# Quarters of the array for four first-layer blocks and three token tiles of an attention and GELU kernel

## The chip, the cores and the metric

The kernel runs on one core of one Trainium2 chip. The metric is the device time of one launch in microseconds; lower is better. A core has several engines, each with a queue of its own that runs in order and waits on semaphores: TensorE (PE; its weight loads are listed apart as PEld) multiplies matrices into the accumulation memory PSUM, ScalarE (ACT) applies functions such as exponential and gelu, VectorE (DVE) does sums, products and copies, GpSimd (POOL) does slower elementwise work and issues some DMAs, and SyncE (SP) issues most DMAs. PSUM has eight banks, and one bank holds 512 float32 columns on 128 partitions.

## The reference: what is computed

Attention over 8 batches, 12 heads, 448 tokens and 64 elements a head, with q and k normalised, and then two layers with a gelu between them on the 3584 tokens of 768 elements:

```python
q_n, k_n = (rmsnorm(q, g_q), rmsnorm(k, g_k))
scores = scale * np.matmul(q_n, k_n.transpose(0, 1, 3, 2))
attn = np.exp(scores - np.max(scores, axis=-1, keepdims=True))
attn = attn / (np.sum(attn, axis=-1, keepdims=True) + 1e-09)
x = np.matmul(attn, v)            # heads side by side: 3584 x 768
h = x @ w_in                      # 768 x 2048
g = 0.5 * h * (1.0 + np.tanh(c * (h + 0.044715 * h * h * h)))
out = g @ w_out                   # 2048 x 768
```

## The kernel before

The batches are worked through one after the other. While ScalarE takes the exponentials of one batch's scores, TensorE is given matmuls of the second layer of earlier batches, so that it always has something to do. For batch b the order on TensorE is: scores, key sums and value products of the six pairs of heads in seven groups, with second-layer matmuls as filling in between (function `attention`); then the first layer of the batch (`first_blocks` and the loop at L856 to L861). The order of the work is written out by hand. Each engine takes its instructions in the order in which the Python code emits them. What other engines have to do for the batches ahead (squares, sums, norms, transposes, loads) hangs on slots in a list `m1`, which the helper `plan` sorts by slot; `after(f)` emits what is due after block f of the first layer.

**The first layer** (`mm1`, L394). The 2048 outputs are 16 blocks of 128. A block is the product of six chunks of 128 inputs (`xT`, 448 tokens wide) with the weights `win`, summed in one PSUM bank. From batch 2 on, `parts` is 2: a block's weights go into the array as two halves of 64 columns, which are separate matmuls of 128 rows by 64 columns (128*64 in the profile) and write partitions 0 to 63 and 64 to 127 of the bank. Blocks are taken in pairs, [0, 1], [2, 3] and so on to [12, 13], with 14 and 15 alone. A pair has a PSUM tile of two banks, named `hh`; a single block has one bank, named `h`. When a pair is complete, one gelu on ScalarE (`gelu`, L415) reads both banks and writes `g`.

There are three such places of two banks. `place` (L283) takes the one that has been free for longest, and `leave` (L289) gives it back in the order of the code; the wait for the reader is a semaphore. Scores (`sc`, L300) use the same three places.

**The second layer** (`mm2`, L426). Tokens of two batches, 896, are seven tiles of 128. A tile has two halves of 384 output columns, each the sum over the 16 blocks of `g` in one bank, `o`. As filling, `parts` is 2 as above. After batch 8, tiles 3 to 6 are left: the loop at L864 runs them with `parts` 1, whole matmuls of 128*128, two halves of a tile one after the other, and ScalarE copies the first half to `osb`, VectorE the second, after which the tile is stored by two DMAs from SP. The second half of tile 6 is done by `last_half` (L466) in two pieces of 256 and 128 columns.

**Other shapes.** Scores use halves of the rows: 64 rows by 128 columns (64*128, L320), two heads of a pair at a time, each into its own bank. The leftover 64 keys of the heads (L310) are the one place with quarters, 64 rows by 64 columns (64*64): four matmuls, the two row halves writing different banks, each with a sum of one term.

Of the kernel before, what the change touches and what calls it, by code (L numbers as in the profile page):

```python
# [8 lines left out]
F32 = mybir.dt.float32  # L9
# [7 lines left out]
def kernel(  # L17
# [11 lines left out]
    nc = tc.nc  # L29
    B, H, S, D = q.shape  # L30
    assert (B, H, S, D) == (8, 12, 448, 64)
    d_model = H * D
# [10 lines left out]
    HP = H // 2  # L43
    CH = 4
    NCH = H // CH
    nf = d_ff // 128
    HD = d_model // 2
# [14 lines left out]
    op = ctx.enter_context(tc.tile_pool(name="op", bufs=3))  # L62
# [30 lines left out]
    win = wts.tile([128, HP, d_ff], BF16)  # L93
    wout = wts.tile([128, nf, d_model], BF16)
# [10 lines left out]
    qT, xT = {}, {}  # L105
    g = gp.tile([128, nf, 2 * S], BF16, tag="g", name="g")
# [20 lines left out]
    def own(j):  # L127
        return slice(64 * j, 64 * j + 64)
# [154 lines left out]
    def place(name):  # L283
        i = unused.pop(0)
        t = spots[i].tile([128, 2, 512], F32, tag="sc", name=name)
        taken.append((t, i))
        return t

    def leave(t):  # L289

        n = next(n for n, (u, _) in enumerate(taken) if u is t)
        unused.append(taken.pop(n)[1])
# [49 lines left out]
    def bank():  # L342
        return ps_o.tile([128, 512], F32, tag="o", name="o")
# [48 lines left out]
    hs1 = {}  # L392

    def mm1(b, fs, cs=range(HP), parts=1, only=None, act=True):  # L394

        if cs[0] == 0 and only in (None, fs[0]):
            if len(fs) > 1:
                hs1[fs[0]] = place("hh")
            else:
                pool, tag = ((ps_m, "mm"), (ps_o, "o"))[fs[0] % 2]  # L400
                hs1[fs[0]] = pool.tile([128, 1, 512], F32, tag=tag, name="h")
        h = hs1[fs[0]]
        for j, f in enumerate(fs):
            m = 128 // parts
            for c in cs if only in (None, f) else ():
                for i in range(parts):
                    nc.tensor.matmul(  # L407
                        h[i * m:(i + 1) * m, j, :S],
                        win[:, c // 2 + NCH * (c % 2), f * 128 + i * m:f * 128 + (i + 1) * m], xT[b][:, c],
                        start=(c == 0), stop=(c == HP - 1),  # L410
                    )
        if cs[-1] == HP - 1 and only in (None, fs[-1]) and act:
            gelu(b, fs)

    def gelu(b, fs):  # L415
        nc.scalar.activation(  # L416
            g[:, fs[0]:fs[0] + len(fs), (b % 2) * S:(b % 2 + 1) * S], hs1[fs[0]][:, :, :S],
            AF.Gelu_apprx_tanh
        )
        if len(fs) > 1:  # L420
            leave(hs1[fs[0]])

    out_v = out.rearrange("(r t) d -> t r d", t=NQ)
    osbs = {}

    def mm2(b, i, half, f, parts=1, home=None, scalar=False):  # L426


        if f == 0:
            osbs["ps"] = home or ps_m.tile([128, 512], F32, tag="mm", name="o")  # L430
            if half == 0:
                osbs[i] = op.tile([128, d_model], F32, tag="osb", name="osb")
        o, osb = osbs["ps"], osbs[i]
        m = 128 // parts
        for j in range(parts):
            nc.tensor.matmul(  # L436
                o[j * m:(j + 1) * m, :HD], g[:, f, i * 128 + j * m:i * 128 + (j + 1) * m],
                wout[:, f, half * HD:(half + 1) * HD],
                start=(f == 0), stop=(f == nf - 1),
            )  # L440
        if f + 1 < nf:
            return
        part = osb[:, half * HD:(half + 1) * HD]
        if b + 1 == B and i + 1 == 2 * S // 128:
            nc.scalar.copy(part, o[:, :HD])
            store(b, i, slice(0, HD), (nc.sync, nc.sync))
        else:
            if scalar or b + 1 == B and half == 0:
                nc.scalar.copy(part, o[:, :HD])  # L449
            else:  # L450
                nc.vector.tensor_copy(part, o[:, :HD])
            if half == 1:
                store(b, i, slice(0, d_model), (nc.sync, nc.sync))

    def store(b, i, cols, engs):

        parts, j = [], i * 128
        while j < (i + 1) * 128:
            m = min(P - j % P, (i + 1) * 128 - j)
            parts.append((-m, j))  # L460
            j += m
        for (m, j), eng in zip(sorted(parts), engs):
            m, r, t = -m, ((b // 2) * 2 + j // S) * P + j % P, j % S // P
            eng.dma_start(out_v[t, r:r + m, cols], osbs[i][j - i * 128:j - i * 128 + m, cols])

    def last_half():  # L466

        i, at = 2 * S // 128 - 1, HD
        for k, (n, pool, tag) in enumerate(((256, ps_o, "o"), (128, ps_m, "mm"))):
            o = pool.tile([128, 512], F32, tag=tag, name="o")  # L470
            for f in range(nf):
                nc.tensor.matmul(  # L472
                    o[:, :n], g[:, f, i * 128:(i + 1) * 128], wout[:, f, at:at + n],
                    start=(f == 0), stop=(f == nf - 1),
                )
            cols = slice(at, at + n)
            (nc.vector.tensor_copy, nc.scalar.copy)[k](osbs[i][:, cols], o[:, :n])
            store(B - 1, i, cols, ((nc.sync, nc.sync), (nc.scalar, nc.sync))[k])
            at += n

    def m2_parts(b):
        tiles = range(3) if b % 2 == 0 else range(3, 7)
        order = [(i, half) for i in tiles for half in range(2)]
        if b == 0:

            order.sort(key=lambda t: t[1])
        return [
            lambda i=i, half=half, f=f, **how: mm2(b, i, half, f, **how)
            for i, half in order for f in range(nf)
        ]  # L490
# [3 lines left out]
    for c in range(NCH):  # L494
        p, o = 2 * c, 2 * c + 1
# [61 lines left out]
    def first_blocks(b, after):  # L557

        mm1(b, [0, 1], range(4), 2)
        mm1(b, [0, 1], [4], 2)  # L560
        mm1(b, [2, 3], range(5), 2, 2)
        pair_products(b, HP - 1, 0)
        pair_recips(HP - 1)
        mm1(b, [2, 3], range(5), 2, 3)
        late = b < 3
        if late:
            mm1(b, [4, 5], range(5), 2, 4)
        pair_products(b, HP - 1, 1)
        pair_x(b, HP - 1)
        after("x")  # L570
        mm1(b, [4, 5], range(5), 2, 5 if late else None)
        for fs in ([0, 1], [2, 3], [4, 5], [14]):
            mm1(b, fs, range(4, HP) if fs == [14] else [5], 2)
            for f in fs:
                after(f)
# [73 lines left out]
    def front(step):  # L649
# [57 lines left out]
        elif name == "o":  # L707
            w_out_part(i // 2, slice(i % 2 * nf // 2, (i % 2 + 1) * nf // 2))
        elif name == "L":
            loads(*divmod(i, 10))  # L710
        elif name in ("Sq", "Sk"):
            square(1, i, n, eng)
        elif name in ("Tq", "Tk"):
            total(1, i, n)
        elif name == "Rs":
            rsqrt(1, slice(0, 2))
        elif name in ("Nq", "Nk"):
            normed(1, i // 10, n, i % 10, eng)
        elif name == "Tp":
            tps["Q", i] = trans(1, i, "q", ps_o, "o")  # L720
            tps["K", i] = trans(1, i, "k", ps_m, "mm")
        elif name in ("Cq", "Ck"):
            (place_q if n == "q" else place_k)(1, i, tps[n.upper(), i], eng)
        elif name in ("GELU", "EXP"):
            nc.scalar.preload_act_table_set(EXP_SET if name == "EXP" else GELU_SET)
        elif name == "mb":
            mm1(0, [0, 1], [i], act=False)
        elif name in ("ma", "mc", "md"):
            fs = [2 * i, 2 * i + 1] if i < 7 else [i + 7]
            cs = {"ma": range(4), "mc": [4], "md": [5] if i < 3 else range(HP)}[name]  # L730
            mm1(0, fs, cs, act=False)
        elif name == "g":
            gelu(0, [2 * i, 2 * i + 1] if i < 7 else [i + 7])
        else:
            raise ValueError(step)
# [44 lines left out]
    m2 = []  # L780
    for b in range(B):
# [67 lines left out]
        def after(f):  # L849
            for fn in m1.get(f, ()):  # L850
                fn()

        if b:
            after(-1)
            first_blocks(b, after)
            for i in range(3, nf // 2 - 1):  # L856
                mm1(b, [2 * i, 2 * i + 1], parts=2)
                after(2 * i)
                after(2 * i + 1)
            mm1(b, [15], parts=2)  # L860
            after(15)  # L861
        m2 += m2_parts(b)
        if b + 1 == B:
            for i, fn in enumerate(m2[:-nf]):  # L864
                fn(**(dict(home=bank()) if i % (2 * nf) == nf else {}))
            last_half()
            break
        nc.scalar.preload_act_table_set(EXP_SET)
# [42 lines left out]
```

## Time and profile before

| | us |
|---|---|
| median of 3 runs | 421.32 |
| lowest and highest run | 420.64, 423.59 |
| profiled execution, from the first instruction to the last (its span) | 418.5 |
| TensorE busy | 407.3 |
| ScalarE busy | 297.7 |
| VectorE busy | 273.7 |
| GpSimd busy | 131.7 |

The profile is of one execution of its own and gives its span; the time of that execution outside the span is not on the page. Times in the profile are in microseconds, mean durations in nanoseconds. A line names an engine, the line of the code, the operation, the tile written and the tiles read, then the shape (rows*columns of the array for matmuls) and how many there were. "Idle before" is the time that the engine stood still ahead of them, with what ended it. The views used here are the page itself, groups of instructions by line and shape, the timeline (instructions in order of time, neighbours of one kind merged), and the chain that ended last, followed back from the last instruction.

### The profile page before, as it was taken

To read this page: it belongs to the slowest core of one execution; us is meant where nothing else is said; L and a number is where in the kernel's file an instruction comes from. 1 tells how busy PE (TensorE), PEld (TensorE's weight loads), DVE (VectorE), ACT (ScalarE), POOL (GpSimd) and SP (SyncE) were. 2 spreads that over 40 slices of the span, in tenths; PEclk is the share of its full clock that TensorE was granted. 3 is DMA by queue.
4 is the path that set the end of the run, shared out by engine and by line. 5 is a ranking of instruction groups with operands and counts; after the bars stand their busy time and mean duration, and the time that the engine had idled before them with its cause. 6 is when DMAs were issued, how large, how long until landed. Compare 5 with 4: busy or idle time off the path is not lost.

```text
span 418.5 us, 9913 instructions
## 1 busy us (share of the span) xinstructions
PE 407.3 (97%) x4120; PEld 249.6 (60%) x4120; DVE 273.7 (65%) x454; ACT 297.7 (71%) x401; POOL 131.7 (31%) x142
## 2 busy tenths in 40 slices
PE   7899899999999999999999999999999999999996
PEld 3244455576655765567655765567655675557664
DVE  5898758899589648881678747786578642782010
ACT  4897787879997787776967778685876558774300
POOL 7897400033200744037500745019500560000000
PEclk9699999999999999999999999999999999999999
DMA  7999999938981499419881398718681161210022
GB/s 191 217 231 230 204 198 228 237 108 178 219 143 39 75 212 199 95 44 187 205 143 39 74 205 156 146 39 158 152 142 39 26 109 40 67 49 0 2 78 76
DMA packets 97870, 54.20 MB, mean 130 GB/s; under 512 B 63776, under 2 KB 94368, under 8 KB 97824
## 3 DMA queue, kind: packets, MB, share of 16 engines
q1 hardware_dynamic: 71424, 41.71, 42.2%
q0 software_dynamic: 26112, 11.80, 22.2%
q8 instruction: 32, 0.52, 0.5%
q14 instruction: 14, 0.11, 0.1%
q10 hardware_dynamic: 288, 0.06, 0.1%
HBM read 45.61 MB, written 11.01 MB: 135 GB/s over the span
## 4 chain that ended last, share of the span: by engine, by line
PE 91%; DVE 4%; ACT 3%; issue 1%; ACTq 0%; DVEq 0%
PE o L436 33%; PE hh L407 29%; PE o L365 12%; PE sc L320 7%; PE h L407 4%; PE sc L310 2%; ACT ex L326 1%; PE w L217 1%; PE ox L365 1%; DVE nrmq L226 1%; DVE nrmk L226 1%; PE o L472 1%; PE tp L238 0%; DVE qT L255 0%; DVE kT L264 0%
## 5 line engine op out<-in xcount | busy, mean ns | idle before, releaser
L436 PE MATMUL o<-wout,g 128*64 128x384 bf16 (+1 forms) x1648 | 155.3, 326 | 0.0
L326 ACT ACTIVATE ex<-sc,shift 128x896 bf16<-128x896 f32 x144 | 135.8, 1012 | 1.7 <-PE sc L320 1.6
L407 PE MATMUL hh<-xT,win 128*64 128x448 bf16 (+1 forms) x1260 | 133.2, 353 | 0.0
L407 PEld LDWEIGHTS <-win 128*64 128x64 bf16 (+1 forms) x1440 | 102.4, 109 | 42.4 <-issue 0.8
L436 PEld LDWEIGHTS <-g 128*64 128x64 bf16 (+1 forms) x1648 | 97.2, 109 | 47.8 <-issue 3.8
L416 ACT ACTIVATE g<-hh 128x896 bf16<-128x896 f32 x56 | 49.9, 918 | 40.6 <-PE hh L407 40.6
L203 DVE TENSOR_REDUCE ss<-sq 128x14 f32<-128x896 f32 (+4 forms) x45 | 47.7, 1081 | 31.7 <-ACT sq L186 20.1
L449 ACT COPY osb<-o 128x384 f32<-128x384 f32 x51 | 24.6, 483 | 50.0 <-PE o L436 49.9
L764 POOL COPY mark<-es 1x1 bf16<-1x1 bf16 x7 | 1.7, 242 | 166.1 <-DVE es L340 152.6
L372 DVE STREAM_TRANSPOSE st<-o 128x448 f32<-128x448 f32 x48 | 31.1, 648 | 25.3 <-PE o L365 25.2
L320 PE MATMUL sc<-qT,kT 64*128 64x448 bf16 x288 | 39.1, 359 | 2.5 <-DVE kT L264 1.5
L340 DVE TENSOR_TENSOR es<-ex 128x896 bf16<-128x896 bf16 x42 | 26.6, 632 | 15.9 <-ACT ex L326 15.9
L226 POOL TENSOR_TENSOR nrmq<-rawq,rinv 112x512 bf16<-112x512 f32 x34 | 35.2, 1050 | 2.8 <-ACT rinv L212 2.6
L380 DVE STREAM_TRANSPOSE rb<-rc 128x448 f32<-128x448 f32 x48 | 31.0, 645 | 1.6
L365 PE MATMUL o<-ex,vb 128*64 128x448 bf16 x252 | 31.2, 353 | 0.1
L226 POOL TENSOR_TENSOR nrmk<-rawk,rinv 128x512 bf16<-128x512 f32 (+1 forms) x33 | 30.9, 952 | 0.0
L279 DVE TENSOR_SCALAR kT<-kT,gcol 128x896 bf16<-128x896 bf16 x19 | 19.6, 1032 | 12.4 <-DMA kT<-nrmk 12.4
L338 DVE TENSOR_TENSOR es<-es,exr 64x896 bf16<-64x896 bf16 x42 | 25.9, 617 | 2.7 <-ACT exr L326 1.3
L340 DVE TENSOR_TENSOR es<-es,ex 128x896 bf16<-128x896 bf16 x42 | 25.6, 609 | 2.7 <-ACT ex L326 0.8
L188 POOL TENSOR_TENSOR sq<-rawq 112x1024 f32<-112x1024 f32 x9 | 17.6, 1951 | 30.9 <-DMA rawq<-in_q_dram 17.4
L390 DVE TENSOR_TENSOR xT<-o,rb 128x448 bf16<-128x448 f32 x42 | 25.9, 616 | 0.9 <-PE o L365 0.4
L320 PEld LDWEIGHTS <-kT 64*128 64x128 bf16 x288 | 10.0, 94 | 24.9 <-issue 17.8
(83 smaller groups left out, 347.2 us busy)
## 6 DMA issues: line engine op xcount, KB each, us to landing
rawq<-in_q_dram SPq DMA_DIRECT2D x48, 224.0 KB, 4.4
rawk<-in_k_dram SPq DMA_DIRECT2D x48, 192.0 KB, 4.6
vb<-in_v_dram POOLq DMA_DIRECT2D x8, 576.0 KB, 11.6
win<-in_moe_w_in_dram POOLq DMA_DIRECT2D x4, 768.0 KB, 14.1
wout<-in_moe_w_out_dram POOLq DMA_DIRECT2D x4, 768.0 KB, 20.2
out_dram<-osb SPq DMA_DIRECT2D x7, 336.0 KB, 3.3
out_dram<-osb SPq DMA_DIRECT2D x8, 288.0 KB, 2.7
out_dram<-osb SPq DMA_DIRECT2D x8, 240.0 KB, 2.5
```

The source lines that it names most:

```text
L203: nc.vector.reduce_sum(stat(ssq[b % 3], b, c, n, j), view(n, sqs[n, b, c], j), axis=AX.X)
L226: eng.tensor_mul(dst.rearrange("p t a d -> p a t d"), view(n, raws[n, b, c], j), r.to_broadcast(list(r.shape) + [D]),)
L320: nc.tensor.matmul(sc[:, a, :S], kT[r, c, 4 * j + t], qT[b][r, hp], start=True, stop=True,)
L326: nc.scalar.activation(dst, sc[:, :, :S], AF.Exp, scale=scale, bias=shift)
L338: nc.vector.tensor_add(es[p], es[p], exrs[b, hp // 2][p])
L340: nc.vector.tensor_add(es, ex[:, 0] if t == 1 else es, ex[:, t])
L365: nc.tensor.matmul(o[a * D:(a + 1) * D], w(a), e[:, a], start=(i == 0), stop=(i + 1 == len(steps)),)
L372: nc.vector.transpose(oas["st"].rearrange("p a b -> p (a b)"), oas[0])
L380: nc.vector.transpose(oas["rb", hp], oas["rc"].to_broadcast([128, S // 32, 32]))
L407: nc.tensor.matmul(h[i * m:(i + 1) * m, j, :S], win[:, c // 2 + NCH * (c % 2), f * 128 + i * m:f * 128 + (i + 1) * m], xT[b][:, c], start= ...
L416: nc.scalar.activation(g[:, fs[0]:fs[0] + len(fs), (b % 2) * S:(b % 2 + 1) * S], hs1[fs[0]][:, :, :S], AF.Gelu_apprx_tanh)
L436: nc.tensor.matmul(o[j * m:(j + 1) * m, :HD], g[:, f, i * 128 + j * m:i * 128 + (j + 1) * m], wout[:, f, half * HD:(half + 1) * HD], start ...
```

## The change

In batches 2 to 8, blocks 8 to 11 are no longer done by `mm1` in halves but by a new function `mm1_quarters`. It places both pairs, [8, 9] and [10, 11], at once. A block pair's matmuls come in two turns. In the first turn the upper 64 rows of the array work for the first block of the pair (its bank) and the lower 64 rows for the second; in the second turn they change over. Each row half is split into two column halves, so that four matmuls of 64*64 stand in the array. The order is: first turn of [8, 9], first turn of [10, 11], second turn of [8, 9] and its gelu, second turn of [10, 11] and its gelu. Ahead of each second turn stands a `nop` on TensorE that waits for the last matmul of the same pair's first turn (`follows`), since the two row halves may not write one bank at the same time. The steps due after each block follow its gelu, in the same order as before.

After batch 8, token tiles 3, 4 and 5 are done by `mm2_quarters` in the same manner: both output halves of a tile have a place of two banks, in the first turn the upper rows (the first 64 of each block of `g`) sum the left columns and the lower rows the right ones, and in the second turn they change over. The order is 3 first, 4 first, 3 second, 5 first, 4 second, 5 second. After the second turn ScalarE copies the left half, VectorE the right half, and the tile is stored. The first half of tile 6 and `last_half` stay as they were.

```diff
+    def follows(later, earlier):
+        tc.add_manual_dep(
+            later.ins, earlier.ins.name,
+            mybir.DependencyInfo(mybir.DependencyClass.Sync, mybir.DependencyReason.DATA),
+            reason="row tiles take turns in a bank",
+        )
+
+    def mm1_quarters(b, fs, after):
+        for f in fs[::2]:
+            hs1[f] = place("hh")
+        last = {}
+        for turn in range(2):
+            for f in fs[::2]:
+                if turn:
+                    follows(nc.tensor.nop(), last[f, 0])
+                for c in range(HP):
+                    for r in range(2):
+                        j = r ^ turn
+                        for i in range(2):
+                            m = (f + j) * 128 + i * 64
+                            ins = nc.tensor.matmul(
+                                hs1[f][own(i), j, :S],
+                                win[own(r), c // 2 + NCH * (c % 2), m:m + 64], xT[b][own(r), c],
+                                start=(c == 0 and turn == 0), stop=(c == HP - 1 and turn == 1),
+                            )
+                        if turn == 0:
+                            last[f, 0] = ins
+                if turn:
+                    gelu(b, [f, f + 1])
+                    after(f)
+                    after(f + 1)
...
+    def mm2_quarters(i, turn):
+        if turn == 0:
+            osbs["q", i] = place("oq")
+        else:
+            follows(nc.tensor.nop(), osbs["turn", i])
+        o = osbs["q", i]
+        for f in range(nf):
+            for r in range(2):
+                j = r ^ turn
+                for m in range(2):
+                    at = i * 128 + m * 64
+                    osbs["turn", i] = nc.tensor.matmul(
+                        o[own(m), j, :HD], g[own(r), f, at:at + 64],
+                        wout[own(r), f, j * HD:(j + 1) * HD],
+                        start=(f == 0 and turn == 0), stop=(f == nf - 1 and turn == 1),
+                    )
+        if turn:
+            osbs[i] = op.tile([128, d_model], F32, tag="osb", name="osb")
+            nc.scalar.copy(osbs[i][:, :HD], o[:, 0, :HD])
+            nc.vector.tensor_copy(osbs[i][:, HD:], o[:, 1, :HD])
+            leave(o)
+            store(B - 1, i, slice(0, d_model), (nc.sync, nc.sync))
...
-            for i in range(3, nf // 2 - 1):
-                mm1(b, [2 * i, 2 * i + 1], parts=2)
-                after(2 * i)
-                after(2 * i + 1)
+            mm1(b, [6, 7], parts=2)
+            after(6)
+            after(7)
+            mm1_quarters(b, [8, 9, 10, 11], after)
+            mm1(b, [12, 13], parts=2)
+            after(12)
+            after(13)
             mm1(b, [15], parts=2)
...
-            for i, fn in enumerate(m2[:-nf]):
-                fn(**(dict(home=bank()) if i % (2 * nf) == nf else {}))
+            for turn, i in ((0, 3), (0, 4), (1, 3), (0, 5), (1, 4), (1, 5)):
+                mm2_quarters(i, turn)
+            for fn in m2[-2 * nf:-nf]:
+                fn()
             last_half()
```

## The prediction

> **What bounds the kernel now.** I start with the head of the page and its slices.
>
> ```profile
> span 418.5 us, 9913 instructions
> PE 407.3 (97%) x4120; PEld 249.6 (60%) x4120; DVE 273.7 (65%) x454; ACT 297.7 (71%) x401; POOL 131.7 (31%) x142
> ...
> PE   7899899999999999999999999999999999999996
> ...
> PEclk9699999999999999999999999999999999999999
> ...
> PE 91%; DVE 4%; ACT 3%; issue 1%; ACTq 0%; DVEq 0%
> ```
>
> TensorE is busy for 407.3 of 418.5 us, at a full granted clock in nearly every slice, and the chain that ended last is 91% TensorE. So only what lengthens or shortens TensorE's own stream reaches the end, unless something makes it wait. The chain in order of time shows how the two changed stages stand in it: first the end of the first layer in batch 6, then the end of the last batch. The columns are start, time up to the next piece, and what ran; `hh` and `h` are first-layer blocks, `o` L436 is the second layer.
>
> ```profile
> 283.49 3.03 PE hh L407 x32
> ...
> 383.47 9.14 PE hh L407 x96
> 392.61 1.13 PE h L407 x12
> 393.74 18.31 PE o L436 x112
> 412.05 2.65 PE o L472 x32
> ```
>
> No other engine stands between them. I call a **slot** the time that one full pass of moving columns takes. In the first layer two matmuls (halves of the array's columns) share a slot: 96 matmuls in 9.14 us are 48 slots of 0.190 us, 32 in 3.03 us are 16 of 0.189. In the last batch's second layer a matmul takes the whole array: 112 slots in 18.31 us, 0.163 each. A slot's 64 columns fewer (384 for 448) save 26.6 ns, 0.416 ns a column; 448 columns are then 186.4 ns and about 2.7 ns of a slot are fixed.
>
> **What the change does to the slots.** It makes the same products with quarters: 64 rows by 64 columns of the array, four matmuls where the first layer had two and the second layer one. Work per slot is equal: blocks 8 to 11 had 4 x 6 x 2 = 48 matmuls in 24 slots, and have 2 turns x 2 pairs x 6 x 4 = 96 quarters, 24 slots if four run side by side. The token tiles 3, 4 and 5 had 96 full matmuls in 96 slots, and have 384 quarters, again 96 slots. So where a slot keeps its length the change gains nothing; 7 x 24 = 168 slots of 448 columns and 96 of 384 are concerned, 264 in all. Do four quarters run together? The kernel has one place with this shape, the leftover keys at L310. From the timeline of TensorE (start, length of the group, count):
>
> ```profile
> 22.43 0.36 PE L365 MATMUL ox<-exr,vr 128*64 128x448 bf16 x2
> 22.71 0.38 PE L310 MATMUL sc<-qT,kT 64*64 64x448 bf16 x4
> ...
> 302.28 0.38 PE L310 MATMUL sc<-qT,kT 64*64 64x448 bf16 x4
> 302.59 0.35 PE L436 MATMUL o<-wout,g 128*64 128x384 bf16 x2
> ...
> 393.01 0.73 PE L407 MATMUL h<-xT,win 128*64 128x448 bf16 x5
> 393.68 0.34 PE L436 MATMUL o<-wout,g 128*128 128x384 bf16 x1
> ```
>
> Four quarters last 0.38 us together, as one pair does, row halves writing two banks at once. So they do, for one group. I take the slot unchanged; what the trace doesn't show is a second group behind the first, and that is what the rivals are about.
>
> **What changing the shape costs.** The same rows price it. From the pair at 22.43 to the quarters at 22.71 are 0.28 us where a slot is 0.19: 0.09 on the way in. From quarters at 302.28 to halves at 302.59 are 0.31: 0.12 on the way out. Each of batches 2 to 8 goes in once, between blocks 7 and 8, and out once, between 11 and 12: 7 x 0.21 = **1.47 us**. The last batch goes from halves to full array today: the last `h` matmul ends at 393.74 and lasts 0.35, so it began at 393.39, and 0.29 lie to 393.68, 0.10 over a slot. After the change it goes from halves to quarters (0.09) and from quarters to full array at tile 6 (0.12, by the row out): **0.11 us** more. Nothing lies beside these: the array is what is waited for.
>
> The Trainium skill, "TensorE: Matmul & The Clock Gate", section "Part 3: Packing small matmuls", says that a weight load overlaps running matmuls only where its group of rows is another. By that rule halves, which share all rows, would show each load between two slots; the rows below have loads of 0.11 us inside slots of 0.19, so the trace disagrees. By the rule a quarter's load would show too, 264 x 0.11 = 29 us and 452; by the rows the sum stays.
>
> ```profile
> L407 PE MATMUL hh<-xT,win 128*64 128x448 bf16 x1176 | 116.6, 353 | 0.0
> ...
> L407 PEld LDWEIGHTS <-win 128*64 128x64 bf16 (+1 forms) x1440 | 102.4, 109 | 42.4 <-issue 0.8
> ...
> 383.34 0.57 PE L407 MATMUL hh<-xT,win 128*64 128x448 bf16 x4
> ```
>
> **The order of loads.** Two pairs last 0.57 us: the fourth matmul started 0.57 - 0.35 = 0.22 after the first, 0.03 beyond a slot. So a half waits about 0.03 us behind its load. If all four quarters wait so, in a row, that is 4 x 0.03 = 0.12 us, inside a slot of 0.19 and one of 0.163. It hides, below the slot; without that cover a slot would be what the loads take.
>
> **The waits added.** A `nop` stands ahead of each second turn: 2 in each of 7 batches and 3 at the end, 17. Behind it on TensorE are all later quarters. It waits for the last matmul of the same pair's first turn, and between them lies a whole turn of another pair or tile: 6 slots (1.1 us) in the first layer, 16 (2.6 us) in the second. A matmul lasts 0.35, so it is over 0.8 us before. I take zero; from the other side, a nop that emptied the array would cost a drain, 0.35 - 0.19 = 0.16 and a step like the 0.12 above, some 0.2 to 0.3 each, 3.4 to 5 us in all.
>
> **What moves beside it.** Pair 8, 9 is complete after 18 of the 24 slots and not after 12, so its gelu starts 6 x 0.19 = 1.1 us later; 10, 11 as before. The ACT timeline of batch 6 shows what hides that (its last two rows are the chain's, in the same columns as above):
>
> ```profile
> 287.41 0.93 ACT L416 ACTIVATE g<-hh 128x896 bf16<-128x896 f32 x1
> ...
> 289.26 0.92 ACT L416 ACTIVATE g<-hh 128x896 bf16<-128x896 f32 x1 [0.49 <-PE hh L407]
> 291.53 0.92 ACT L416 ACTIVATE g<-hh 128x896 bf16<-128x896 f32 x1 [1.35 <-PE hh L407]
> 292.35 0.62 ACT L186 ACTIVATE sq<-rawq 112x512 f32<-112x512 f32 x1
> 293.80 0.92 ACT L416 ACTIVATE g<-hh 128x896 bf16<-128x896 f32 x1 [0.83 <-PE hh L407]
> 294.62 0.62 ACT L186 ACTIVATE sq<-rawq 112x512 f32<-112x512 f32 x1
> 295.14 0.57 ACT L186 ACTIVATE sq<-rawk 128x448 f32<-128x448 f32 x1
> 296.07 0.92 ACT L416 ACTIVATE g<-hh 128x896 bf16<-128x896 f32 x1 [0.37 <-PE hh L407]
> ...
> 297.90 1.28 ACT L868 ACT_TABLE_LOAD   x1
> ...
> 297.17 0.67 PE sc L320 x6
> 297.85 4.02 PE o L436 x48
> ```
>
> Gelu 8, 9 moves from 291.53 to about 292.8; its square and gelu 10, 11 end near 295.2, two squares near 296.3, and gelu 12, 13 starts near 296.4 for 296.07, 0.2 of that being TensorE's own delay. The idle times in brackets (1.35, 0.83, 0.37) take up the rest. Some 0.3 us could reach the table load and the first exponentials, and TensorE then has 48 second-layer matmuls (4.0 us) to do before it needs a bank of scores again. Zero; at worst 0.3 x 6 batches = 1.8 us. The steps planned on slots 8 to 11 (loads and transposes on SP, squares on ACT, sums and gains on DVE) keep their order on every queue. The early start of pair 10, 11 needs its two banks 1.1 us sooner; the gelu of 4, 5 that frees them began at 287.41. At the end, tiles 3 and 4 are stored 16 slots later, tile 5 when it was, and tile 6 with the last half, which sets the end, is untouched.
>
> **Sum.** 1.47 + 0.11 = 1.58 us on a span of 418.5, 420.1. The page gives no time outside the span; the median of the runs, 421.32, lies 2.8 above, and I keep that distance: **422.9 us**, 0.4% slower. Runs of before spread over 420.64 to 423.59, so about 1% is what a measurement can tell from no change.
>
> **Rivals.**
> *Supply.* TensorE's queue has to deliver 8 instructions (four loads, four matmuls) a slot where halves take 4 and the full array 2. The fastest run of load and matmul in the trace is at the very end:
>
> ```profile
> 414.19 0.50 PE L472 MATMUL o<-wout,g 128*128 128x128 bf16 x6
> ...
> q8 instruction: 32, 0.52, 0.5%
> ```
>
> With 0.22 us for one (the last ends at 414.69), six in 0.50 are 0.056 apart, which is also what 128 columns take, so it is a ceiling and no proof. Four at 0.056 are 0.224: 0.035 more in 168 slots and 0.061 in 96, 5.9 + 5.9 = 11.7 us, 434.6 with the switches. What a long stretch shows is only halves of the second layer, 0.163 / 2 = 0.081 a pair: 0.325 a slot would be 22.8 + 15.6 us and 461. Fetching (32 packets, 0.52 MB in the span) would have to double its rate there. For it: nothing in the trace is as dense. Against: the four matmuls of L310 last 0.38 together, each about 0.35 by the row further below, so they start within 0.03. Decides from a pair above 0.041 (tiles) or 0.047 (blocks). Chance 0.14.
> The skill's same page, section "Back-to-back issue gap", gives about 81 ns for a sustained load and matmul at 128 columns, by which it would be the 461; the trace's 0.056 disagrees.
> *The waits bite.* Each nop empties the array: 422.9 + 3.4 to 5 = 426.3 to 428. Against: 6 or 16 slots between. Chance 0.08.
> *Quarters don't pair up.* When they accumulate, the two row halves take turns, or loads are not hidden: the change doesn't do what it says. A load of 0.11 shown in each slot is 264 x 0.11 = 29 us, 452; full turns double the slots, 168 x 0.19 + 96 x 0.163 = 47.5 us, 470. L310 never accumulates, so nothing excludes it, but its two banks took full writes. Chance 0.08.
> *Faster.* The fixed part of a slot goes, four streams filling each other's gaps: 2.7 ns, and 4 more, because these rows show 64-row matmuls 4 ns shorter (349 for 353):
>
> ```profile
> L320 PE MATMUL sc<-qT,kT x288: 346/349/567, 10.6 to 372.9; 64*128 64x448 bf16 x144
> ...
> 368.05 0.55 PE L320 MATMUL sc<-qT,kT 64*128 64x448 bf16 x4
> ```
>
> 264 x 6.7 ns = 1.8 us, which beats the switches only from 6 ns a slot. With switches paid it is 421.1; if quarters also take their places as the halves before them run out, 419.5. Against: two pairs of row halves take 0.55 in all, so they step by 0.20, no less than halves of columns. Chance 0.08.
> My forecast has the other 0.62.
>
> **Range and chances.** 420.0 leaves out about 0.05 below. Above, the waits and part of the supply case (0.05 a pair: 4 x 0.05 = 0.2 a slot, 1.8 + 3.6 = 5.4 us) lie inside 431; about 0.14 lies beyond. Within 1% (417.1 to 425.5) are my forecast, nearly all of the faster case and a little of the others: 0.71. Slower by over 1%: 0.26. Faster by over 1% needs 16 + 6 ns off each slot: 0.03.
>
> **What would show it.** TensorE's 24 slots of blocks 8 to 11 take 4.54 us before and should take 4.75 with both switches; four quarters start within 0.1 us of each other; 96 slots of tiles take 15.6 us. Idle TensorE ahead of a quarter, released by TensorE itself, would show the nops; slots of 0.2 or more with no releaser show the supply; pairs of quarters one behind the other show that they don't pair up. Wrong would be the sum if the first quarter behind a second-turn boundary or the exponentials after the table load left TensorE idle.

## The result and the profile after

The changed kernel takes 424.42 us (median of 17 runs) where before took 422.13 in runs beside it: a ratio of 1.0057, with a 95% interval of 1.0036 to 1.0078, or 1.5 to 3.3 us more. The forecast was 1.6 more. The page of the changed kernel, by the lines that were read before:

```profile
span 423.4 us, 11161 instructions
PE 411.2 (97%) x4744; PEld 243.2 (57%) x4744; DVE 277.4 (66%) x454; ACT 297.4 (70%) x401; POOL 132.6 (31%) x142
...
PEclk9689999999999999999999999999999999999999
...
q8 instruction: 37, 0.61, 0.6%
```

TensorE is still what is busy, at the same clock but for one slice, with 624 more matmuls (4744 for 4120) and 3.9 us more of busy time. Instructions were fetched in 37 packets where before had 32 (the last line). The spans of the two profiled executions lie 4.9 us apart, more than the runs; so a span isn't the thing to compare, and the stages are. The chain that ended last (start, time up to the next piece, what ran), first in before for batches 5 and 6, then in the changed kernel for the same batches and for the end (L437 is `mm1_quarters`, L501 `mm2_quarters`):

```profile
238.61 9.14 PE hh L407 x96
...
286.90 9.14 PE hh L407 x96
```

```profile
244.73 4.66 PE hh L437 x96
249.39 2.39 PE hh L407 x24
...
290.94 2.33 PE hh L407 x24
293.27 4.66 PE hh L437 x96
297.93 2.39 PE hh L407 x24
...
398.52 15.72 PE oq L501 x384
414.25 2.71 PE o L470 x16
416.95 2.65 PE o L530 x32
```

Blocks 6 to 13 took 9.14 us and take 2.33 + 4.66 + 2.39 = 9.38: 0.24 more. The batch as a whole, from 238.61 to 286.90, was 48.29 us and is 48.54 (244.73 to 293.27): 0.25 more. So nothing is added or given back anywhere else in a steady batch. The end was 18.31 + 2.65 = 20.96 and is 15.72 + 2.71 + 2.65 = 21.08: 0.12 more. Together 7 x 0.25 + 0.12 = **1.87 us** that the trace shows to be the change's.

The timeline of TensorE shows where the 0.24 lies (start, length of the group, count):

```profile
292.70 0.57 PE L407 MATMUL hh<-xT,win 128*64 128x448 bf16 x4
293.20 0.38 PE L437 MATMUL hh<-xT,win 64*64 64x448 bf16 x4
...
293.20 0.57 PE L437 MATMUL hh<-xT,win 64*64 64x448 bf16 x7
...
297.38 0.55 PE L437 MATMUL hh<-xT,win 64*64 64x448 bf16 x8
297.86 0.38 PE L407 MATMUL hh<-xT,win 128*64 128x448 bf16 x2
...
297.86 0.57 PE L407 MATMUL hh<-xT,win 128*64 128x448 bf16 x4
```

The last half began 0.57 - 0.35 = 0.22 after 292.70, at 292.92; the first quarters came 0.28 later, 0.09 over a slot. Four of them last 0.38 together. The second group started 0.57 - 0.35 = 0.22 after the first, 0.02 or 0.03 late. On the way out two groups of four in 0.55 step by 0.55 - 0.35 = 0.20 at the most, so the last started near 297.57, and the halves came 0.29 later: 0.10 over a slot, and their next pair again came 0.57 - 0.35 = 0.22 later, 0.02 or 0.03 late. That is the whole addition. In between, 96 quarters in 4.66 us are 24 slots of 0.189 and the switch out. No line shows TensorE waiting for a `nop`.

### The profile page after: what moved, and what is told of

Read it like the earlier page. It is cut to its first block, busy times and chain, and to the rows that moved or that the text cites. A ratio compares the mean times of both kernels' runs of the same rounds, so it can differ in the third digit from the quotient of the medians.

```text
span 423.4 us, 11161 instructions
## 1 busy us (share of the span) xinstructions
PE 411.2 (97%) x4744; PEld 243.2 (57%) x4744; DVE 277.4 (66%) x454; ACT 297.4 (70%) x401; POOL 132.6 (31%) x142
## 4 chain that ended last, share of the span: by engine, by line
PE 83%; DVE 6%; ACT 3%; POOL 3%; issue 2%; DMA 1%; SPq 0%; DVEq 0%; POOLq 0%; ACTq 0%
PE o L470 26%; PE hh L407 19%; PE o L365 11%; PE sc L320 7%; PE hh L437 7%; PE h L407 4%; PE oq L501 4%; PE w L217 2%; PE sc L310 1%; DVE ss L203 1%; PE ox L365 1%; POOL nrmk L226 1%; POOL nrmq L226 1%; DMA rawq<-in_q_dram 1%; DVE es L340 1%
## 5 line engine op out<-in xcount | busy, mean ns | idle before, releaser
L470 PE MATMUL o<-wout,g 128*64 128x384 bf16 (+1 forms) x1552 | 139.7, 326 | 0.0
L470 PEld LDWEIGHTS <-g 128*64 128x64 bf16 (+1 forms) x1552 | 87.9, 110 | 41.5 <-issue 3.7
L407 PE MATMUL hh<-xT,win 128*64 128x448 bf16 (+1 forms) x924 | 102.7, 353 | 0.0
L407 PEld LDWEIGHTS <-win 128*64 128x64 bf16 (+1 forms) x1104 | 74.7, 109 | 39.2 <-issue 3.3
L483 ACT COPY osb<-o 128x384 f32<-128x384 f32 x48 | 23.2, 484 | 39.4 <-PE o L470 39.3
L437 PE MATMUL hh<-xT,win 64*64 64x448 bf16 x672 | 33.1, 350 | 0.0
L279 DVE TENSOR_SCALAR kT<-kT,gcol 128x896 bf16<-128x896 bf16 x19 | 22.5, 1187 | 12.8 <-DMA kT<-nrmk 12.8
L340 DVE TENSOR_TENSOR es<-es,ex 128x896 bf16<-128x896 bf16 x42 | 26.9, 640 | 2.7 <-ACT ex L326 0.8
L437 PEld LDWEIGHTS <-win 64*64 64x64 bf16 x672 | 19.0, 107 | 13.6 <-issue 2.5
```

The lines of the kernel that those rows point to most:

```text
L340: nc.vector.tensor_add(es, ex[:, 0] if t == 1 else es, ex[:, t])
L407: nc.tensor.matmul(h[i * m:(i + 1) * m, j, :S], win[:, c // 2 + NCH * (c % 2), f * 128 + i * m:f * 128 + (i + 1) * m], xT[b][:, c], start= ...
L437: ins = nc.tensor.matmul(hs1[f][own(i), j, :S], win[own(r), c // 2 + NCH * (c % 2), m:m + 64], xT[b][own(r), c], start=(c == 0 and turn == ...
L470: nc.tensor.matmul(o[j * m:(j + 1) * m, :HD], g[:, f, i * 128 + j * m:i * 128 + (j + 1) * m], wout[:, f, half * HD:(half + 1) * HD], start ...
```

## The experiments

Times are medians; "a steady batch" is read in the traces from the last leftover-key matmuls of one batch to those of the next, from batch 4 on, where before has 48.29 us and the changed kernel 48.53.

| kernel | us | ratio to before, interval | steady batch |
|---|---|---|---|
| changed | 424.42 | 1.0057 (1.0036 to 1.0078) | 48.53 |
| only blocks | 424.28 | 1.0058 (1.0039 to 1.0078) | 48.53 |
| only tiles | 422.12 | 1.0017 (0.9995 to 1.0040) | 48.29 |
| eight blocks | 424.32 | 1.0052 (1.0029 to 1.0076) | 48.80 |
| two switches more | 428.19 | 1.0139 (1.0113 to 1.0164) | 49.62 |
| turns adjacent | 428.06 | 1.0142 (1.0115 to 1.0170) | 49.07 |
| scores in quarters | 421.48 | 0.9979 (0.9962 to 0.9997) | 48.13 |
| scores in quarters by leftovers | 419.45 | 0.9946 (0.9921 to 0.9970) | 48.08 |

My theory was that only a change of the array's shape costs, and that a quarter slot, a `nop` and the later gelu are free. The rivals were a cost per quarter slot, a cost per `nop`, and a later ScalarE queue.

**Both kernels once more.** No edit.

> The kernel before, once more, for a second profile: how much of the 4.9 us between the spans of the two profiles (418.5 and 423.4) is one execution against another. My theory: a batch of steady state lasts 48.29 us again (from the first of the 96 matmuls of blocks 6 to 13 to that of the next batch), while the start, up to block 6 of batch 2, and batch 3 differ by a microsecond or two from the first profile. Rival (the change itself made batch 3 late): here batch 3 has no stall of TensorE, as in the first profile of before.

> The changed kernel once more. My theory, switches of the array's shape alone: a steady batch lasts 48.53 to 48.54 us again, and the 1.3 us that TensorE stood idle in batch 3 ahead of key sums and value products are of that one execution and come out otherwise here. Rival, a later ScalarE queue: the idle time of 1.3 us in batch 3 stands again at the same place.

One run each took 422.1 and 424.19 us, with steady batches of 48.28 and 48.53. The first batch's last leftover keys started at 29.45 and 32.04 us in the two profiles of before, and at 31.40 and 30.90 in those of the changed kernel: the start alone moves by 2.6 us from one execution to the next. The stall (a longer time in which TensorE waits) that the expectations put in batch 3 lies in the pass from batch 3's last leftover keys to batch 4's. This pass was longer than a steady batch by 0.69 and 1.54 us in before, by 2.03 and 2.12 in the changed kernel. TensorE's rows there, first of before's second profile and then of the changed kernel's first:

```profile
165.53 0.76 PE L365 MATMUL o<-ex,vb 128*64 128x448 bf16 x6 [0.81 <-DVE st L372]
```

```profile
164.97 0.38 PE L365 MATMUL o<-es,ones 128*64 128x448 bf16 x2 [0.45 <-DVE es L338]
...
167.29 0.76 PE L365 MATMUL o<-ex,vb 128*64 128x448 bf16 x6 [0.81 <-DVE st L372]
```

I expected the changed kernel's stall to come out otherwise the second time, and it didn't (0.54 and 0.81). But 0.81 of it stood in the second profile of before too, so the rival's statement that before has no stall is wrong as well. The chain leads back over VectorE's sums and a square on GpSimd to a load of `rawq`. GpSimd's square began 29.2 and 29.1 us after those leftover keys of batch 3 in before, 29.8 and 29.9 in the changed kernel, and 29.7 with only the tiles changed, where the first layer of batch 3 is as before. So this does not follow the first layer's quarters. Nor does the length of the pass: it was 1.8 us over a steady batch with only the blocks changed and 1.2 with only the tiles, but also 2.03 and 1.65 in the two kernels at the end of this section, which have nothing of the change.

**Blocks alone, tiles alone.**

The blocks alone, against the changed kernel:

```diff
-            for turn, i in ((0, 3), (0, 4), (1, 3), (0, 5), (1, 4), (1, 5)):
-                mm2_quarters(i, turn)
-            for fn in m2[-2 * nf:-nf]:
-                fn()
+            for i, fn in enumerate(m2[:-nf]):
+                fn(**(dict(home=bank()) if i % (2 * nf) == nf else {}))
```

The tiles alone, against the changed kernel:

```diff
-            mm1(b, [6, 7], parts=2)
...
-            mm1_quarters(b, [8, 9, 10, 11], after)
-            mm1(b, [12, 13], parts=2)
...
+            for i in range(3, nf // 2 - 1):
+                mm1(b, [2 * i, 2 * i + 1], parts=2)
+                after(2 * i)
+                after(2 * i + 1)
```

> Only the first-layer blocks 8 to 11 in quarters, the last token tiles as before. Theory (switches): 7 x 0.25 = 1.7 us over before, a ratio of 1.004; the last three tiles 0.1626 us a slot and 0.10 for their one switch. Rival (the tiles cost most): at most 0.5 us over before.

> Only the last three token tiles in quarters, the first layer as before. Theory (switches): 0.11 to 0.14 us over before, a ratio of 1.000, steady batches of 48.29 us. Rival (the quarters of the tiles or their later stores cost something beside): 0.5 us or more over before, and the last store issued later against the last matmul.

The blocks alone are 0.58% over before, as much as the changed kernel within the intervals (the expected 1.004 is at the low end of theirs); the steady batch is the changed kernel's. The tiles alone cannot be told from before (the interval holds 1). Their traces give the end by itself: from the last leftover keys to the last matmul 45.94 us in before, 46.18 with the blocks alone, 46.06 with the tiles alone and 46.31 in the changed kernel. So tiles cost 0.12 and one batch of blocks 0.24, and the two add up.

**Twice the quarter slots.**

```diff
-            mm1(b, [6, 7], parts=2)
...
-            mm1_quarters(b, [8, 9, 10, 11], after)
-            mm1(b, [12, 13], parts=2)
...
+            mm1_quarters(b, [6, 7, 8, 9], after)
+            mm1_quarters(b, [10, 11, 12, 13], after)
```

> Eight blocks (6 to 13) in quarters, two calls one behind the other, so twice the quarter slots with the same two switches a batch. Theory (only a change of the array's shape costs): a steady batch of 48.53 us as in the changed kernel, the time within 0.5 us of it. Rival (each quarter slot costs a little, or each nop): twice the addition, a steady batch of 48.78, 1.7 us over the changed kernel.

The time is that of the changed kernel, as my theory had it, but a steady batch is 48.80, the rival's number. That the times agree is partly luck: in the profiles three steady passes are 0.27 longer each, and the pass with the stall, from batch 3 to 4, is 0.73 shorter (49.83 for 50.56), which is no more than it differs between two executions of before. The last pass, from batch 7 to 8, is 48.47 with the same eight blocks, 0.06 below the changed kernel's; there ScalarE has no squares to take for later batches. In the others TensorE waits for ScalarE, by the chain that ended last:

```profile
204.62 0.99 ACT ex L326
205.61 0.80 issue
206.41 1.02 ACT ex L326
207.43 0.04 issue
207.47 0.38 PE sc L310 x4
```

The late gelus push back the exponentials, and the leftover keys wait for a place in PSUM. TensorE's idle time there is only 0.14 us, because the matmul before counts as busy for its full 0.35. By the starts of the matmuls, set beside those of the last pass, the leftover keys come 0.21 late and the scores just behind the first layer 0.11, which is the whole difference of 0.32. So neither slots nor nops cost; the rival's size came out by another way, the later ScalarE queue, which in the changed kernel's own steady batches is still covered. Why the last pass is 0.06 below the changed kernel's is open.

**Two more switches a batch.**

```diff
-    def mm1_quarters(b, fs, after):
+    def mm1_quarters(b, fs, after, between=None):
...
         for turn in range(2):
+            if turn and between:
+                between()
             for f in fs[::2]:
...
-            mm1_quarters(b, [8, 9, 10, 11], after)
-            mm1(b, [12, 13], parts=2)
+            mm1_quarters(b, [8, 9, 10, 11], after, lambda: mm1(b, [12, 13], parts=2))
```

> The changed kernel with blocks 12 and 13, still in halves, put between the first and the second turns of blocks 8 to 11: the same quarter slots and the same nops, but the array goes in and out of quarters twice a batch. Theory (switches): a steady batch longer by another 0.21 to 0.25, 48.75 to 48.78 us, 7 x 0.23 = 1.6 us over the changed kernel. Rival (slots or nops cost): 48.53, nothing over it.

In the last pass, without squares, a batch is 48.78: 0.25 over the changed kernel, for two switches, as expected. In the steady ones it is 49.62, 0.84 more than that, and TensorE's row says why: ScalarE again, now with three gelus close behind each other at the end of the first layer.

```profile
209.91 0.38 PE L310 MATMUL sc<-qT,kT 64*64 64x448 bf16 x4 [0.53 <-ACT ex L326]
```

The row's idle time is 0.53 us, and 0.06 more stands at a score just ahead; the matmuls before them count as busy for their full 0.35, so part of each wait doesn't show as idle. By the starts of the matmuls, set beside those of the last pass, the score comes 0.22 late and the leftover keys 0.62 more: the whole 0.84.

**Each second turn directly behind the first.**

```diff
-        for turn in range(2):
-            for f in fs[::2]:
+        for f in fs[::2]:
+            for turn in range(2):
...
-            for turn, i in ((0, 3), (0, 4), (1, 3), (0, 5), (1, 4), (1, 5)):
+            for turn, i in ((0, 3), (1, 3), (0, 4), (1, 4), (0, 5), (1, 5)):
```

> Each second turn directly behind its own first turn, so that each of the 17 nops waits for a matmul just issued. Theory: here the wait bites, 0.2 to 0.3 us each: a steady batch 0.4 to 0.6 us longer than the changed kernel's 48.53, 3.4 to 5 us over it in all, and TensorE shows gaps of 0.4 to 0.5 us between the turns. Rival (TensorE keeps the order of its matmuls by itself, the nop costs nothing wherever it stands): 48.53 and no gap.

The chain now falls apart at each `nop`:

```profile
244.56 1.29 PE hh L437 x24
245.90 2.49 PE hh L437 x48
248.43 1.33 PE hh L437 x24
249.76 2.39 PE hh L407 x24
...
400.49 2.75 PE oq L501 x64
403.29 5.42 PE oq L501 x128
408.76 5.42 PE oq L501 x128
414.23 2.79 PE oq L501 x64
```

From 244.56 to 249.76 are 5.20 us for 4.66: two nops, 0.27 each. From 400.49 to 414.23 + 2.79 are 16.53 for 15.72: three, again 0.27. Seventeen make 4.6 us; the time rose by 3.6 over the changed kernel's 424.42, in runs on another occasion (each against the runs of before beside it, 5.5 and 2.3 us, by 3.2). In the profiles the pass with the stall, from batch 3 to 4, is 1.0 us shorter (49.59 for 50.56), which would make up the difference. The price is as forecast. Of each 0.27 only 0.07 shows as idle time, because the matmul before counts as busy, so the gaps of 0.4 to 0.5 us that were expected are not in the trace. In the changed kernel the price isn't paid: there the other pair's turn lies between, and the groups of quarters follow each other at a plain slot across each `nop`.

**Scores in quarters.** This kernel has nothing of the change. The scores' row halves of before are split by columns too, so that the leftover keys behind them need no change of shape.

```diff
-                nc.tensor.matmul(
-                    sc[:, a, :S], kT[r, c, 4 * j + t], qT[b][r, hp], start=True, stop=True,
-                )
+                for o in (own(0), own(1)):
+                    nc.tensor.matmul(
+                        sc[o, a, :S], kT[r, c, 4 * j + t, o], qT[b][r, hp], start=True, stop=True,
+                    )
```

> The kernel before, with the scores' row halves (64 by 128) also split into column halves, so that scores are quarters like the leftover keys that follow them. Nothing of the change is in it. Theory (only changing shape costs, quarter slots are free): the step from scores to leftover keys falls from 0.28 to 0.19, 0.09 us at each of 24 places less a little where TensorE waits anyway, about 2 us less than before, a ratio of 0.995, a steady batch of 48.0 us. Rival (quarters cost by themselves, more instructions): the same as before or slower.

It is faster, by half of what was expected: a steady batch 48.13 for 48.29 (one pass, from batch 6 to 7, was 48.67, with a wait that leads back to a load of `rawk`). Of the three places in a batch, two give 0.10 each, but at the third TensorE then waits 0.08 us for VectorE's key sum, and three of the four groups without leftover keys became 0.02 longer (0.69 for 0.67 us), which I had not reckoned with.

**Only by the leftover keys.**

```diff
+                for o in (own(0), own(1)) if b and (hp, t) in near else (slice(0, 128),):
...
+    near = {n for group in GROUPS if "r" in [t for _, t in group] for n in group}
```

> The kernel before, with the scores in quarters only in the groups that also hold leftover keys, from batch 2 on; the four groups without keep their row halves, which cost 0.02 us less a group. Theory: a steady batch of 48.07 to 48.09 us, 0.2 under before and 0.05 under the version with all scores in quarters, 7 x 0.2 = 1.4 us under before, a ratio of 0.9966. Rival (the 0.02 is not there or comes back as a wait): 48.13, a ratio of 0.998.

48.08, as expected, and the fastest kernel here: 419.45 us, a ratio of 0.9946 (0.9921 to 0.9970). Its rows show the step that is gone:

```profile
253.99 0.57 PE L321 MATMUL sc<-qT,kT 64*64 64x448 bf16 x8
254.40 0.36 PE L310 MATMUL sc<-qT,kT 64*64 64x448 bf16 x4
254.69 0.35 PE L437 MATMUL o<-wout,g 128*64 128x384 bf16 x2
```

The second group of scores began 0.57 - 0.35 = 0.22 after 253.99, the leftover keys 0.19 behind that, a plain slot; in before the same step was 0.28. The trace accounts for 7 x 0.2 = 1.4 us; the medians lie 2.8 apart with 0.3 to 0.8% in the interval, 1.3 to 3.3 us. What the rest of the 2.8 is, if it is more than scatter, is open.

## Why the prediction was right, point by point

- **Slots keep their length.** Shown: 24 slots of 0.189 in the blocks, 15.72 us for 96 slots of tiles (15.61 at 0.1626, the rest the switch out). Four quarters start within 0.01 us of each other and follow without a gap, with 8 instructions a slot, so the rival of supply falls: load and matmul came every 0.041 us through 15.7 us.
- **Switches.** The mechanism was right and the size short. Terms: in 0.09 and out 0.12, 0.21 a batch; the trace has 0.25. Up to the first halves behind the quarters the forecast holds: from the last half ahead of them to these, less a slot, are 297.86 - 292.92 - 0.19 = 4.75 us, which is what was forecast for the 24 slots with both switches. Missing is the next pair of halves, 0.02 or 0.03 late behind the way out. Before shows it too, behind the row that I took the price from:

```profile
302.59 0.52 PE L436 MATMUL o<-wout,g 128*64 128x384 bf16 x4
```

  A matmul of L436 lasts 0.33, so the second pair started 0.19 behind the first, where a slot of 384 columns is 0.163. The leftover keys thus held the whole price, 0.09 + 0.12 + 0.03 = 0.24, and I read two of its three parts. That the 0.12 is in the changed kernel 0.10 on the way out and 0.02 at the second group of quarters fits this, since the leftover keys are one group; it is a reading of the rows and has no experiment of its own. The end: 0.11 forecast, 0.12 measured.
- **The order of loads.** It hides, as taken, but not for the reason given: the 0.03 us between two halves was taken for a wait behind a load, and four quarters, each with a load of its own, show no such step.
- **Waits.** Zero, as taken; 0.27 each where they bite, inside the 0.2 to 0.3 that was worked out.
- **ScalarE.** Gelu 8, 9 was to start 1.1 us later and the last pair 0.3 at the most. The rows after:

```profile
293.30 0.92 ACT L450 ACTIVATE g<-hh 128x896 bf16<-128x896 f32 x1 [0.49 <-PE hh L407]
296.85 0.92 ACT L450 ACTIVATE g<-hh 128x896 bf16<-128x896 f32 x1 [2.63 <-PE hh L437]
...
300.36 0.92 ACT L450 ACTIVATE g<-hh 128x896 bf16<-128x896 f32 x1 [0.29 <-PE hh L407]
```

  From gelu 6, 7 to gelu 8, 9 are 3.55 us where 2.27 were (289.26 to 291.53): 1.28 later, 1.1 of it the slots. Gelu 12, 13 still waits for TensorE (0.29 for 0.37), so nothing is handed on to the exponentials. The cover held, and the two kernels with more late gelus show how thin it is.
- **Not pairing up, and faster.** Neither: the four of a group start together, and a slot's fixed part is still there (0.189 for 448 columns and 0.1626 for 384, as before).
- **Sum.** 1.58 us forecast, 1.87 by the trace, 2.3 by the medians with an interval of 1.5 to 3.3. The 0.4 between the last two lies within the interval. The stall between batches 3 and 4 was longer in both profiles of the changed kernel than in both of before, but in the two scores kernels, which have nothing of the change, it was 2.03 and 1.65, so nothing ties it to the change.

## What to carry to other kernels

Splitting a full pass of the array into quarters neither gains nor costs by itself; what costs is each change of shape, 0.24 us here for going in and out once, where TensorE is never idle. So count the changes of shape along the queue and give neighbours the same shape, as with the scores and the leftover keys, before asking what a shape does. A wait for a result just issued cost 0.27 us a time, and nothing with six slots of other work between; and work that is completed later should be followed to the engine that takes it over, since the cover there may be a few tenths.

## What was not expected of the hardware

In most first-layer blocks the second half of a pair starts 0.03 us behind the first (four in 0.57 us, 0.35 each), while four quarters start together, group after group. This isn't a property of halves: the halves of blocks 12 and 13 behind the quarters start together too (the first row below: four in 0.55, so 0.20 from the first to the last, hardly more than a slot), and so do the two of the second layer at 302.59 (0.35 us for both). What sets the 0.03 is open. And loads of weights for all four quarters (about 0.107 us each) stay hidden in slots of 0.163 us, though both column halves of a row half load through the same rows.

```profile
298.07 0.55 PE L407 MATMUL hh<-xT,win 128*64 128x448 bf16 x4
...
L437 PEld LDWEIGHTS <-win 64*64 64x64 bf16 x672 | 19.0, 107 | 13.6 <-issue 2.5
...
L501 PEld LDWEIGHTS <-g 64*64 64x64 bf16 x384 | 11.1, 107 | 4.6 <-issue 0.4
...
L501 PE MATMUL oq<-wout,g 64*64 64x384 bf16 x384 | 15.8, 323 | 0.0
```
